# Loading k as float32 beside q, casting it on VectorE and ScalarE, and giving chunks 14 to 17 to transposing transfers

## The chip, the cores and the metric

The kernel runs on one core of a Trainium2 chip. The core has a matrix engine (TensorE, PE in the profile, with its weight loads shown as PEld), a vector engine (VectorE, DVE), a scalar engine (ScalarE, ACT), a general engine that here also issues the loads (GpSimd, POOL), and SyncE (SP), which issues stores and transposing transfers. Sixteen DMA engines move the data. The metric is the device time of one execution in microseconds (us).

## The reference

Inputs: q, k and v of shape (8 batches, 8 heads, 576 positions, 64) and two weight matrices, 512 x 2048 and 2048 x 512, all float32. A retention layer (attention without softmax, with a decay for each head) is followed by a feed-forward block with the Mish activation.

```python
scores = scale * np.matmul(q, k.transpose(0, 1, 3, 2))          # scale = 1/sqrt(64)
gamma = 1.0 - 2.0 ** (-5.0 - np.arange(H))
Dmat = np.where(rel >= 0, gamma[:, None, None] ** rel, 0.0)     # rel = i - j
ret = scores * Dmat
x = np.matmul(ret, v)           # then (batch, position, head * 64): 4608 x 512
h = x @ w_in
out = (h * np.tanh(softplus(h))) @ w_out                        # 4608 x 512, float32
```

## The kernel before

**Chunks and tiles.** The 4608 positions are cut into 36 chunks of 128. Chunks 0 to 7 are the first 128 positions of each batch. From chunk 8 on they come for two batches at a time: three chunks of 128 of the one, three of the other, and one chunk that joins the last 64 positions of both (chunks 14, 21, 28, 35). Four chunks make a tile of 512 positions, so there are nine tiles, t = 0 to 8. Matrix products take bfloat16 inputs and sum in float32.

**Retention by chunk.** A decay is split into a factor for the row (`gq`, which scales q) and one for the column (`gv`, which scales v), so that inside a chunk only a 0/1 mask remains and everything before the chunk goes through a running state of k times v. A chunk n >= 8 passes these steps:

- `load` (L253): GpSimd issues the loads of q (into `qraw`, float32), k (into half of `qks`; this transfer casts float32 to bfloat16 on the way) and v (into `vraw`, float32). One semaphore serves every eighth load, and a load waits until the one eight places before it has landed.
- P, `step_p` (L271): VectorE multiplies q by `gq` and writes bfloat16 into the other half of `qks`.
- V, `step_v` (L276): GpSimd multiplies v by `gv` into `vs`.
- T, `step_t` (L282): `qks` is transposed into `qkT`. For n < NPE (18) TensorE makes eight 128 x 128 transposes into a PSUM buffer `sc`, and ScalarE copies them out (L288, L289). From chunk 18 on a transposing transfer issued by SyncE does it (L291).
- S, `step_s` (L294): TensorE makes the scores of the chunk, VectorE masks them into `sm` (L305).
- `state` (L319): TensorE adds one chunk's k times v to the state (L333), VectorE copies it out as `ssb` (L336). For the first chunk of a batch the k comes from `k0`, which `load_k0` (L247) loads with a cast by the transfer, in eight buffers.
- O, `step_o` (L343): TensorE applies state and scores; VectorE copies the result into the tile's input `xT` (L362).

**Feed-forward.** `g1` (L366) makes one of sixteen 128-wide slices of the hidden layer for a tile: four matmuls into `hp`, a PSUM buffer of which there are two, then Mish on ScalarE. `g2` (L375) makes a quarter of the second product for one chunk, four matmuls. Its sum is in `hp` or in `ops`, a single buffer. `store` (L420) copies it to `res` on VectorE (L422), and SyncE stores it.

**Order.** Every engine works through its own instructions in the order in which the program writes them; nothing is reordered. The first chunks (tiles 0 and 1) have their own path up to about 50 us. Then a loop over u = 0 to 23 (L529) runs the slices of tile 1 with the steps of chunks 8 to 13 between them: P at u = 0, 4, 8, 12, 16, 20 and T at u = 3, 7, 11, 15, 19, 22. The main loop (L563) then runs t = 2 to 9 with sixteen iterations i, in two halves of eight (w = 0 to 7), each half for two chunks n and n + 1, n = 12, 14, 16 and so on: S of the two at w = 0, O at w = 4. P and T of the chunks that follow stand in two places. While they are transposed by TensorE, P of chunks n + 2 and n + 3 is at w = 1 and 3 and T at w = 5 and 6. When they go by transfer, P of n + 4 and n + 5 is at w = 7, and T of n + 2 and n + 3 at w = 0 and 1 of the next half, eight iterations before the S that needs it. In tile t = 2 an iteration has four matmuls of `g1`, and every second one four of `g2`; from t = 3 on it has four of each. Loads run up to five chunks ahead (PF, L47 to L48).

Of the kernel before, what the change touches and what calls it, by code (L numbers as in the profile page):

```python
# [10 lines left out]
F32 = mybir.dt.float32  # L11
BF16 = mybir.dt.bfloat16
AX = mybir.ActivationFunctionType
OP = mybir.AluOpType
# [3 lines left out]
def kernel(  # L18
# [18 lines left out]
    nc = tc.nc  # L37
    B, H, S, D = q.shape
    assert (B, H, S, D) == (8, 8, 576, 64)
    P = 128  # L40
    NP = H // 2
# [2 lines left out]
    nF = d_ff // P  # L44
    KC = d_model // P
    NCH = 4
    NPE = 18  # L47
    PF = 5  # L48


# [11 lines left out]
    consts = ctx.enter_context(tc.tile_pool(name="consts", bufs=1))  # L62
    wpool = ctx.enter_context(tc.tile_pool(name="weights", bufs=1))
    first = ctx.enter_context(tc.tile_pool(name="first", bufs=1))
    io = ctx.enter_context(tc.tile_pool(name="io", bufs=PF))
    tok = ctx.enter_context(tc.tile_pool(name="tok", bufs=5))
    tr = ctx.enter_context(tc.tile_pool(name="tr", bufs=4))
    xp = ctx.enter_context(tc.tile_pool(name="xp", bufs=2))
    gp = ctx.enter_context(tc.tile_pool(name="gp", bufs=2))
    op = ctx.enter_context(tc.tile_pool(name="op", bufs=4))  # L70
# [8 lines left out]
    live = {}  # L79
# [72 lines left out]
    for h in range(H):  # L152
        nc.vector.tensor_scalar(dmask[:, h, :], dist, lg[h], None, op0=OP.mult)
    ex = consts.tile([P, 5, H], F32)
    gq = consts.tile([P, 5, H], F32)
    gv = consts.tile([P, 5, H], F32)
    warm = consts.tile([P, 1], F32)

# [10 lines left out]
    st_sb = {}  # L169
    xts = {}  # L170
    k0 = {}
    v0s = {}


# [7 lines left out]
    def f_transpose(t, g, i, parts):  # L182

        name = ("qb", "kb")[i]
        out_t = first.tile([P, H, P], BF16, name=name + "T", bufs=2)
        n = 8 // len(parts)
        moves = []
        for j, (pool, tname, copy) in enumerate(parts):
            tp = pool.tile([P, 2, 8, P] if tname == "sc" else [P, 8, P], BF16, name=tname)
            tp = (tp[:, 0] if tname == "sc" else tp)[:, 0:n]  # L190
            for r in range(n):
                if t == 1:
                    mix = fst[1][name, "mix", g][:, n * j + r]
                    nc.tensor.transpose(tp[:, r, :], mix.rearrange("p x d -> p (x d)"), ident)
                else:
                    for x in range(2):
                        nc.tensor.transpose(tp[ds(64 * x, 64), r, :],
                                            fst[0][name][:, 2 * g + x, ts(n * j + r, D)], ident)
            moves.append((copy, out_t.rearrange("p h (g r) -> p h g r", r=8)[:, :, :, ds(n * j, n)],
                          tp.rearrange("p r (g h) -> p h g r", h=H)))  # L200
        for copy, to, src in moves:
            copy(to, src)
        fst[t][name, g] = out_t
# [41 lines left out]
        engine.tensor_tensor(v0s[n], v0[n], gv[:, 0, :].unsqueeze(2).to_broadcast([P, H, D]), op=OP.mult)  # L245

    def load_k0(b):  # L247
        k0[b] = first.tile([P, H, D], BF16, name="k0", bufs=B)
        nc.gpsimd.dma_start(out=k0[b], in_=k[b, :, 0:P, :].rearrange("h p d -> p h d"))

    def load(n):  # L253
        if n >= n_chunks:
            return
        b, c = chunks[n]
        qr = io.tile([P, H, D], F32, name="qraw")
        vr = io.tile([P, H, D], F32, name="vraw", bufs=7)
        qks = io.tile([P, 2, H, D], BF16, name="qks", bufs=9)
        live[n] = {"q": qr, "v": vr, "qks": qks}  # L260
        for t, src in ((qr, q), (qks[:, 1], k), (vr, v)):
            if c < 4:
                nc.gpsimd.dma_start(  # L263
                    out=t, in_=src[b, :, ds(P * c, P), :].rearrange("h p d -> p h d"))
            else:
                for e in range(2):
                    nc.gpsimd.dma_start(  # L267
                        out=t[ds(64 * e, 64)],
                        in_=src[b + e, :, ds(512, 64), :].rearrange("h p d -> p h d"))

    def step_p(n):  # L271
        c = chunks[n][1]
        nc.vector.tensor_tensor(live[n]["qks"][:, 0], live[n]["q"],  # L273
                                gq[:, c, :].unsqueeze(2).to_broadcast([P, H, D]), op=OP.mult)

    def step_v(n):  # L276
        c = chunks[n][1]
# [4 lines left out]
    def step_t(n):  # L282
        flat = live[n]["qks"].rearrange("p i h d -> p (i h d)")
        qk = tr.tile([P, 2, NP, P], BF16, name="qkT", bufs=5)
        if n < NPE:
            tp = ps_sc.tile([P, 4 * NP, P], BF16, name="sc")[:, 0:2 * NP]
# [32 lines left out]
    def state(upto):  # L319

        if upto >= n_chunks or done[0] > state_of[upto]:
            return False
        b, c = states[done[0]]
        done[0] += 1
        if c == 0:
            ks, vs = k0[b], v0s[b]
            st_ps[b] = ps_st.tile([P, NP, 64], F32, name="st")
        else:
            ks, vs = live[index[b, c]]["qks"][:, 1], live[index[b, c]]["vs"]
        st = st_ps[b]  # L330
        for p in range(NP):
            for e in range(2):
                nc.tensor.matmul(st[ds(64 * e, 64), p, :], lhsT=ks[:, 2 * p + e, :], rhs=vs[:, 2 * p + e, :],  # L333
                                 start=(c == 0 and p == 0), stop=True, skip_group_check=True)
        ssb = tr.tile([P, 2, NP, 64], BF16, name="ssb", bufs=6)
        nc.vector.tensor_tensor(  # L336
            ssb.rearrange("p e n d -> p e (n d)"),
            st.rearrange("p n d -> p (n d)").unsqueeze(1).to_broadcast([P, 2, NP * 64]),
            diag.unsqueeze(2).to_broadcast([P, 2, NP * 64]), op=OP.mult)
        st_sb[b, c] = ssb  # L340
        return True
# [51 lines left out]
    def stores():  # L393
        while ready:
            store(*ready.pop(), nc.vector.tensor_copy)
# [24 lines left out]
    def store(t, s, ops, copy):  # L420
        ot = op.tile([P, d_model], F32, name="res")
        copy(ot, ops)  # L422
        b, c = chunks[NCH * t + s]
        if c < 4:
            nc.sync.dma_start(out=out[ds(b * S + P * c, P), :], in_=ot)
        else:
            for e in range(2):
                nc.sync.dma_start(out=out[ds((b + e) * S + 512, 64), :], in_=ot[ds(64 * e, 64), :])

    def att(n, steps):  # L430
        if n >= n_chunks:
            return
        for step in steps:
            {"P": step_p, "V": step_v, "T": step_t, "S": step_s, "O": step_o}[step](n)
# [65 lines left out]
    for i in range(nF):  # L500
        for step in steps.get(i, "").split():
            n = int(step[1])
# [17 lines left out]
    def more_loads(upto):  # L520
        for _ in range(2):
            if queued[0] <= upto:
                load(queued[0])
                queued[0] += 1
# [3 lines left out]
    att(N0, "PV")  # L528
    for u in range(24):  # L529
        j, w = divmod(u, 4)  # L530
        if w == 0 and j > 0:
            att(N0 + j, "PV")
            if j < 5:
                if j == 4:
                    load_k0(2)
                load(N0 + j + 3)
            else:
                more_loads(N0 + j + PF)
                load_k0(3)
        elif w == 1 and j > 0:  # L540
            if j > 3:
                state(N0 + j - 1)
            if j < 5:
                att(N0 + j - 1, "S")
            if j < 4:
                state(N0 + j - 1)
            if j > 1:
                att(N0 + j - 2, "O")
            if j == 4:
                state(N0 + j - 1)  # L550
            stores()
        elif w == 2 and 0 < j < 5:
            f_state(1, j - 1, nc.vector)
        elif (w == 3 and j < 5) or (w == 2 and j == 5):
            att(N0 + j, "T")
        stores()
        if u < nF:
            g1(1, u)
        else:
            g2(1, u - nF)  # L560


    for t in range(2, nT + 1):  # L563
        for i in range(nF):
            n, w = NCH * (t + 1) + i // 8 * 2, i % 8
            if t in (3, 4) and i in (4, 12):
                load_k0(2 * t - 2 + i // 8)
            by_pe = n + 2 < NPE
            if w == 0:
                stores()  # L570
                state(n + 1)
                att(n, "S")
                att(n + 1, "S")
            if w == 4:
                state(n + 3)
                stores()
                att(n, "O")
                att(n + 1, "O")
                state(n + 3)
            if by_pe and w in (1, 3):  # L580
                att(n + 2 + w // 2, "P")
            if w in (0, 1):
                att(n + 2 + w, "V")
            if w in (4, 5):
                more_loads(n + w - 2 + PF)
            if w - (5 if by_pe else 0) in (0, 1):
                att(n + 2 + (w == 1 or w == 6), "T")
            if w == 7 and n + 4 >= NPE:
                att(n + 4, "P")
                att(n + 5, "P")  # L590
            stores()
            if t < nT:
                g1(t, i)
            if t == 2:
                if i % 2:
                    g2(1, 8 + i // 2)
            elif t < nT or i < 12:
                g2(t - 1, i)
# [32 lines left out]
```

## Time and profile before

| what | value |
|---|---|
| runs | 312.92 us median of 3 (312.32 to 312.98) |
| the profiled execution | 313.61 us, of which the span of the profile is 311.9 us |
| PE busy | 300.3 us, 96% of the span |
| DVE, ACT, POOL busy | 137.1, 110.7, 143.6 us |
| granted TensorE clock | full in every slice |
| DMA | 42.85 MB in 73642 packets |
| loads by GpSimd (q0) | 48640 packets, 27.27 MB, 61.1% of 16 engines' span |
| transfers by SyncE (q1) | 24832 packets, 15.08 MB, 23.3% |

Times in the views count from the start of the span. A group's line gives the source line, engine, operation, what is written and read, and the number of instructions; a timeline's line gives start, duration and the idle time before. "DMA to landing" is the time from the issue of a transfer to the semaphore that tells of its end.

### The profile page before, as it was taken

Reading aid. Unit: us, or ns where it says so; the run is one execution under the profiler, and the core shown is the slowest. Engines: PE = TensorE matmul, PEld = TensorE weight load, DVE = VectorE, ACT = ScalarE, POOL = GpSimd, SP = SyncE. Lnnn points to the kernel's source line nnn. Section 1 sums busy time; section 2 is a strip of 40 time slices with the busy share of each in tenths; the row PEclk is TensorE's granted clock in tenths of the full one; section 3 lists DMA queues with packets and bytes.
Section 4 is the critical chain, followed back from the end, with each engine's and each line's share of the span. In section 5 each row is a group of like instructions: output and inputs, shape, how many; then the busy total and the mean of one; then the engine's idle time right before and its main releaser. Section 6 shows DMA issues by size and latency. Waiting matters only on the chain.

```text
span 311.9 us, 5809 instructions
## 1 busy us (share of the span) xinstructions
PE 300.3 (96%) x2429; PEld 152.3 (49%) x2468; DVE 137.1 (44%) x200; ACT 110.7 (36%) x183; POOL 143.6 (46%) x178
## 2 busy tenths in 40 slices
PE   7769999999999999999999999999999999999995
PEld 3444554555465554545454444545454544444444
DVE  4723455778637635443434453535354332001111
ACT  4546345671453623233333333232323333333300
POOL 8578849989985976274726262612010000000000
PEclk9999999999999999999999999999999999999999
DMA  7999999999995999999996949371504100010031
GB/s 177 234 206 205 220 208 221 256 171 175 232 203 96 148 181 191 155 195 146 179 178 116 189 88 218 77 144 37 101 36 101 36 34 36 35 34 34 36 101 68
DMA packets 73642, 42.85 MB, mean 137 GB/s; under 512 B 58640, under 2 KB 64528, under 8 KB 73616
## 3 DMA queue, kind: packets, MB, share of 16 engines
q0 software_dynamic: 48640, 27.27, 61.1%
q1 hardware_dynamic: 24832, 15.08, 23.3%
q8 instruction: 19, 0.31, 0.5%
q10 hardware_dynamic: 144, 0.13, 0.1%
q14 instruction: 7, 0.06, 0.1%
HBM read 38.80 MB, written 9.44 MB: 155 GB/s over the span
## 4 chain that ended last, share of the span: by engine, by line
PE 92%; issue 2%; DMA 2%; POOL 2%; DVE 0%; ACT 0%; POOLq 0%; ACTq 0%
PE hp L371 39%; PE ops L386 30%; PE hp L386 4%; PE sc L301 3%; PE st L333 3%; DMA gT<-in_v_dram 2%; PE hp L403 2%; PE sc L353 2%; PE sc L358 2%; PE sc L288 1%; PE st L403 1%; PE ops L403 1%; PE hp L414 1%; POOL gT L106 1%; POOL vb L222 1%
## 5 line engine op out<-in xcount | busy, mean ns | idle before, releaser
L371 PE MATMUL hp<-xT,w_in_t 128*128 128x512 bf16 (+1 forms) x562 | 141.3, 373 | 2.2 <-DVE xT L239 0.8
L373 ACT ACTIVATE gT<-hp 128x512 bf16<-128x512 f32 (+1 forms) x148 | 86.8, 586 | 156.4 <-PE hp L371 144.2
L386 PE MATMUL ops<-w_out_t,gT 128*128 128x512 bf16 x430 | 110.1, 379 | 0.4
L371 PEld LDWEIGHTS <-w_in_t 128*128 128x128 bf16 x592 | 55.1, 98 | 61.9 <-DVE xT L239 1.3
L386 PEld LDWEIGHTS <-gT 128*128 128x128 bf16 x496 | 48.2, 98 | 58.1 <-issue 0.8
L422 DVE COPY res<-ops 128x512 f32<-128x512 f32 x28 | 19.3, 688 | 82.7 <-PE ops L386 79.7
L279 POOL TENSOR_TENSOR vs<-vraw,gv 128x512 bf16<-128x512 f32 x28 | 30.3, 1096 | 51.8 <-PE sc L358 37.6
L336 DVE TENSOR_TENSOR ssb<-st,diag 128x512 bf16<-128x512 f32 x32 | 21.9, 685 | 47.2 <-PE st L333 47.2
L305 DVE TENSOR_TENSOR sm<-sc,mask 128x1024 bf16<-128x1024 f32 x28 | 33.0, 1215 | 6.2 <-PE sc L301 6.2
L263 POOL DMA_DIRECT2D qraw<-in_q_dram x24 | 21.8, 910 | 12.8 <-DVE qks L273 9.6
L263 POOL DMA_DIRECT2D vraw<-in_v_dram x24 | 21.8, 908 | 2.9 <-DMA vpair<-in_v_dram 1.5
L263 POOL DMA_DIRECT2D qks<-in_k_dram x24 | 21.8, 906 | 1.3 <-DMA w_out_t<-in_moe_w_out_dram 0.9
L273 DVE TENSOR_TENSOR qks<-qraw,gq 128x512 bf16<-128x512 f32 x28 | 20.2, 758 | 0.0
L362 DVE CAST xT<-sc 128x512 bf16<-128x512 f32 x24 | 15.3, 680 | 0.0
L386 PE MATMUL hp<-w_out_t,gT 128*128 128x512 bf16 x61 | 14.7, 379 | 0.2
L289 ACT COPY qkT<-sc 128x1024 bf16<-128x1024 bf16 x10 | 10.1, 1010 | 8.0 <-PE sc L288 8.0
L215 DVE TENSOR_TENSOR sm<-sc,dmask 128x1024 bf16<-128x1024 f32 x8 | 9.4, 1220 | 5.0 <-PE sc L211 5.0
L353 PE MATMUL sc<-qkT,ssb 128*64 128x128 bf16 (+1 forms) x224 | 9.5, 213 | 0.0
L358 PE MATMUL sc<-sm,vs 128*64 128x128 bf16 x192 | 9.4, 219 | 0.0
L301 PE MATMUL sc<-qkT 64*128 64x128 bf16 x224 | 9.0, 218 | 0.0
L403 PEld LDWEIGHTS <-gT 128*128 128x128 bf16 x64 | 5.8, 98 | 6.5
L267 POOL DMA_DIRECT2D qraw<-in_q_dram x8 | 5.6, 706 | 7.3 <-DVE qks L273 7.3
(103 smaller groups left out, 192.0 us busy)
## 6 DMA issues: line engine op xcount, KB each, us to landing
out_dram<-res SPq DMA_DIRECT2D x31, 256.0 KB, 3.0
qraw<-in_q_dram POOLq DMA_DIRECT2D x24, 256.0 KB, 6.0
vraw<-in_v_dram POOLq DMA_DIRECT2D x24, 256.0 KB, 6.8
qks<-in_k_dram POOLq DMA_DIRECT2D x24, 128.0 KB, 6.4
w_in_t<-in_moe_w_in_dram POOLq DMA_DIRECT2D x4, 512.0 KB, 11.1
w_out_t<-in_moe_w_out_dram POOLq DMA_DIRECT2D x4, 512.0 KB, 9.8
gT<-in_q_dram SPq DMA_DIRECT2D x4, 256.0 KB, 4.9
gT<-in_k_dram POOLq DMA_DIRECT2D x8, 128.0 KB, 6.3
```

The source lines that it names most:

```text
L263: nc.gpsimd.dma_start(out=t, in_=src[b, :, ds(P * c, P), :].rearrange("h p d -> p h d"))
L273: nc.vector.tensor_tensor(live[n]["qks"][:, 0], live[n]["q"], gq[:, c, :].unsqueeze(2).to_broadcast([P, H, D]), op=OP.mult)
L279: nc.gpsimd.tensor_tensor(vs, live[n]["v"], gv[:, c, :].unsqueeze(2).to_broadcast([P, H, D]), op=OP.mult)
L301: nc.tensor.matmul(sc[:, e, p, :], lhsT=qk[r, 1, p, :], rhs=qk[r, 0, p, :], start=True, stop=True)
L305: nc.vector.tensor_tensor(sm.rearrange("p e n i -> p (e n) i"), sc.rearrange("p e n i -> p (e n) i"), m.unsqueeze(1).to_broadcast([P, 2 * ...
L336: nc.vector.tensor_tensor(ssb.rearrange("p e n d -> p e (n d)"), st.rearrange("p n d -> p (n d)").unsqueeze(1).to_broadcast([P, 2, NP * 64 ...
L353: nc.tensor.matmul(ot[ds(64 * e, 64), p, ds(i0, iw)], lhsT=st_sb[bb, cc][:, e, p, :], rhs=qk[:, 0, p, ds(i0, iw)], start=(i0 == 0 and p == ...
L371: nc.tensor.matmul(hp[:, cols], lhsT=w_in_t[:, c, ts(f, P)], rhs=xts[t][:, c, cols], start=(c == 0), stop=(c == KC - 1))
L373: nc.scalar.activation(gts[t][:, f, cols], hp[:, cols], AX.Mish)
L386: nc.tensor.matmul(ops, lhsT=gts[t][:, f, ts(s, P)], rhs=w_out_t[:, f, :], start=(f == 0), stop=(f == nF - 1))
L403: nc.tensor.matmul(outs[0, s], lhsT=gts[0][:, f, ts(s, P)], rhs=w_out_t[:, f, :], start=(f == 0), stop=(f == nF - 1))
L422: copy(ot, ops)
```

## The change

The loads of k no longer cast. For chunks from 8 on, k lands as float32 beside q in one tile `qkraw`, and P on VectorE multiplies both in one instruction: q by `gq`, k by ones, from a table `gqk`; the result is the bfloat16 `qks`. For the first chunks, k lands as float32 in `k0r`, and ScalarE casts it into `k0` (`cast_k0`). NPE goes from 18 to 14: the transposes of chunks 14 to 17 become transfers, their T moves to w = 0 and 1, and all P of chunks from 14 on are made ahead (14 and 15 at u = 23, the others at w = 7). The transposed tiles of the first chunks share the ring of `qkT`.

```diff
-    NPE = 18
+    NPE = 14
...
-    gq = consts.tile([P, 5, H], F32)
+    gqk = consts.tile([P, 5, 2, H], F32)
+    nc.vector.memset(gqk, 1.0)
+    gq = gqk[:, :, 0, :]
...
-        out_t = first.tile([P, H, P], BF16, name=name + "T", bufs=2)
+        out_t = tr.tile([P, 2, NP, P], BF16, name="qkT", bufs=5).rearrange("p i n t -> p (i n) t")
...
     def load_k0(b):
-        k0[b] = first.tile([P, H, D], BF16, name="k0", bufs=B)
-        nc.gpsimd.dma_start(out=k0[b], in_=k[b, :, 0:P, :].rearrange("h p d -> p h d"))
+        k0r[b] = first.tile([P, H, D], F32, name="k0r", bufs=2)
+        nc.gpsimd.dma_start(out=k0r[b], in_=k[b, :, 0:P, :].rearrange("h p d -> p h d"))
+
+    def cast_k0(b):
+        k0[b] = first.tile([P, H, D], BF16, name="k0", bufs=3)
+        nc.scalar.copy(k0[b], k0r[b])
...
-        qr = io.tile([P, H, D], F32, name="qraw")
+        qkr = io.tile([P, 2, H, D], F32, name="qkraw")
         vr = io.tile([P, H, D], F32, name="vraw", bufs=7)
-        qks = io.tile([P, 2, H, D], BF16, name="qks", bufs=9)
-        live[n] = {"q": qr, "v": vr, "qks": qks}
-        for t, src in ((qr, q), (qks[:, 1], k), (vr, v)):
+        live[n] = {"qk": qkr, "v": vr}
+        for t, src in ((qkr[:, 0], q), (qkr[:, 1], k), (vr, v)):
...
     def step_p(n):
         c = chunks[n][1]
-        nc.vector.tensor_tensor(live[n]["qks"][:, 0], live[n]["q"],
-                                gq[:, c, :].unsqueeze(2).to_broadcast([P, H, D]), op=OP.mult)
+        qks = io.tile([P, 2, H, D], BF16, name="qks", bufs=7)
+        nc.vector.tensor_tensor(qks.rearrange("p i h d -> p (i h) d"),
+                                live[n]["qk"].rearrange("p i h d -> p (i h) d"),
+                                gqk[:, c].rearrange("p i h -> p (i h)").unsqueeze(2).to_broadcast([P, 2 * H, D]),
+                                op=OP.mult)
+        live[n]["qks"] = qks
...
     for u in range(24):
         j, w = divmod(u, 4)
+        if u in (3, 12):
+            cast_k0(u // 12)
...
         elif (w == 3 and j < 5) or (w == 2 and j == 5):
             att(N0 + j, "T")
+        elif w == 3:
+            for n in (NPE, NPE + 1):
+                att(n, "P")
...
+    cast_at = {12: 2, 14: 3, 18: 4, 20: 5, 22: 6, 24: 7}
...
-            by_pe = n + 2 < NPE
+            if w == 2 and n in cast_at:
+                cast_k0(cast_at[n])
...
-            if by_pe and w in (1, 3):
-                att(n + 2 + w // 2, "P")
...
-            if w - (5 if by_pe else 0) in (0, 1):
-                att(n + 2 + (w == 1 or w == 6), "T")
-            if w == 7 and n + 4 >= NPE:
+            if w in (0, 1):
+                att(n + 2 + w, "T")
+            if w == 7:
                 att(n + 4, "P")
                 att(n + 5, "P")
```

More of the change, by code (lines that the diff above doesn't have):

```diff
@@ L171 @@
     k0 = {}
+    k0r = {}
     v0s = {}
```

## The prediction

> **What bounds the kernel now.** I read the page first, then the waits of TensorE, then the timeline of TensorE where the transposes stand, and then the transfers, because both halves of the change end in the transfers.
>
> ```profile
> PE 300.3 (96%) x2429; PEld 152.3 (49%) x2468; DVE 137.1 (44%) x200; ACT 110.7 (36%) x183; POOL 143.6 (46%) x178
> ...
> PE 92%; issue 2%; DMA 2%; POOL 2%; DVE 0%; ACT 0%; POOLq 0%; ACTq 0%
> ```
>
> TensorE is the bound, and the chain that ended last runs through it for 92% of the span. The waits of TensorE say that almost nothing holds it up today:
>
> ```profile
> PE st L236 <- POOL vb L222: 1.7, 1, 1.7
> ```
>
> It is the longest of six waits, and all lie in the first 20 us, which the change leaves alone. So each instruction that leaves TensorE is a gain at its full issue time, and each new wait of TensorE is a loss at its full length. Here is one half of tile 2, with the eight transposes of a chunk between matmuls:
>
> ```profile
> 101.31 0.61 PE L288 MATMUL sc<-ident,qks 128*128 128x128 bf16 x8
> 101.75 1.03 PE L371 MATMUL hp<-xT,w_in_t 128*128 128x512 bf16 x4
> ```
>
> **What is removed.** From the first transpose at 101.31 to the next matmul at 101.75 are 0.44 us. Four chunks make 4 x 0.44 = 1.8 us off the path. Their four ScalarE copies (L289, 1.01 us each) were beside other work, so they bring nothing. This is the whole gain.
>
> **P on VectorE.** P doubles from 512 to 1024 elements. L273 takes 0.68 us now; the nearest row for 1024 elements is L305 with 1.22 us, so I add 0.53 us for each of 28, 15 us in all on an engine that is 44% busy. By itself that costs nothing while VectorE has idle time before its next copy; where it hasn't I count it below. One L273 took 1.53 us, at 58.56, while GpSimd's V ran from 58.05 for 1.49 us instead of 1.07; so 2.1 us is the upper bound for a P that meets a V.
>
> [...]
>
> **Casts on ScalarE.** The nearest row is the ScalarE cast of L222, two in 1.14 us, so 0.57 us each, eight in all. Six stand in the main loop, where ScalarE idles over a microsecond between Mish instructions. The first is worse placed, at u = 3, ahead of the copy of chunk 8's transposes, which ran from 54.14 to 55.15; its S starts at 55.71. With 0.57 us more, the copy ends at 55.72, and I count 0.2 us (0 to 0.4).
>
> **Loads of k.** They now land 256 KB instead of 128 KB. What that costs is read where loads queue up behind each other, by issue plus time to landing of q, k and v of chunk 9:
>
> ```profile
> L263 POOL DMA_DIRECT2D qraw<-in_q_dram x1: 922/922/922, 38.8 to 38.8; - x1
> ...
> DMA to landing us min/median/max: 11.8/11.8/11.8
> ...
> L263 POOL DMA_DIRECT2D qks<-in_k_dram x1: 884/884/884, 40.6 to 40.6; - x1
> ...
> DMA to landing us min/median/max: 10.8/10.8/10.8
> ...
> L263 POOL DMA_DIRECT2D vraw<-in_v_dram x1: 882/882/882, 43.0 to 43.0; - x1
> ...
> DMA to landing us min/median/max: 9.5/9.5/9.5
> ```
>
> q lands at 50.6, k at 51.4, v at 52.5, and the next q (issued 45.4, 8.4 us) at 53.8: the cast k takes 0.8 us of the queue, a float32 load about 1.2. So I add 0.4 us for each k. The bounds are 0.45 above, and below zero beneath, since the read stays at 256 KB and the cast's small packets go. I stay with 0.4, because the rows of q and v are the same transfer. Between 35 and 76 us the queue is never empty. The k of chunk 15 was issued at 71.3 and took 4.8 us, so it landed at 76.1; ahead of it, itself included, are eight k of chunks and three `k0`, so it now lands at 76.1 + 11 x 0.4 = 80.5.
>
> [...]
>
> **P of chunks 14 and 15, moved to u = 23.** They now stand on VectorE ahead of the copy of the last sum that `g2` left in `hp`:
>
> ```profile
> 76.67 0.68 DVE L362 CAST xT<-ops 128x512 bf16<-128x512 f32 x1
> 79.70 0.69 DVE L422 COPY res<-hp 128x512 f32<-128x512 f32 x1 [2.35 <-ACT qkT L289]
> ```
>
> The idle 2.35 us would just hold two P. But chunk 15's waits for its k until 80.5, ends at 81.7, and the copy then ends at 82.3. Its `hp` is the one that the second `g1` of tile 2 needs at 80.34 + 0.86 = 81.2. TensorE waits 1.1 us (0 to 1.9, the upper end with a P that meets a V). The mask, `ssb`, and the store on SP queue behind the same P; O comes four iterations later and still finds them done.
>
> **Four more transposing transfers.** What such a pair costs beside loads, and without:
>
> ```profile
> L291 SPq DMA_TRANSPOSE qkT<-qks x2: 1231/2160/3090, 108.0 to 111.3; - x2
> ...
> DMA to landing us min/median/max: 9.5/10.4/11.3
> ...
> L291 SPq DMA_TRANSPOSE qkT<-qks x2: 1259/1273/1287, 204.3 to 205.7; - x2
> ...
> DMA to landing us min/median/max: 3.2/3.3/3.5
> ```
>
> The later of chunks 18 and 19 lands at 111.3 + 11.3 = 122.6, so the pair takes 14.6 us from the first issue. Two halves on (issues at 123.9 and 125.4, the later 11.0 us to landing) it takes 12.5, then (140.1 and 141.6, 9.4) 10.9, and with no load about, at 204.3, 205.7 + 3.2 - 204.3 = 4.6. The first two pairs are the nearest rows, since loads stand as thick from 80 to 104 us; the bounds are 10.9 and 14.6, and 4.6 if the lighter packets free the queue.
>
> Now the room. A half of tile 2 is short: S of chunks 12 and 13 starts at 79.79, of 14 and 15 at 93.15, of 16 and 17 at 106.61. On SP the first transfer waits behind the store whose copy ends at 82.3, so it is issued at about 82.4, and the pair lands at 95.0 to 97.0. The second of the two S, 0.3 us after the first, would start at 93.45 - 0.9 (one chunk pair's transposes gone) + 1.3 (the waits so far) = 93.85. TensorE waits 1.2 to 3.1 us; I take 2.2. For chunks 16 and 17 the store ahead comes after P of 16 and 17, whose last k is itself late; I put the issue at about 95.4, so landing at 107.9 to 110.0, against 106.9 - 1.8 + 3.5 = 108.6: 0 to 1.4 us, 0.6 taken. Chunks 18 and 19 have 15 us already today (S at 122.78) and are the tightest after that; there TensorE is late by as much as the transfers are, so I take nothing, with 1.5 us as the upper bound. Later pairs meet fewer loads and have 15.7 us.
>
> The rest costs nothing: the `gqk` memset is 0.06 us on VectorE (L127's row), while the start waits for loads until 17 us; the shared `qkT` ring and the smaller `qks` and `k0` rings are read out two steps before they come round. Of the casts, the second finds its k 0.8 us early (landed at 62.1, plus six times 0.4; ScalarE is there at 65.3), and the fourth, at about 96 us, is behind a load of 85.3 + 14 x 0.4 = 90.9, before the transfers take their share. I count nothing for them; late, they hold Mish and so TensorE, and they belong to the worst case below.
>
> **The sum.** -1.8 + 0.2 + 1.1 + 2.2 + 0.6 = +2.3 us. Against the profiled execution's 313.61 us that is 315.9; that execution lies 0.7 us over the runs' median of 312.92, so for the median 315.2.
>
> **Rivals.** *The transfers are hidden, and the gain stands (faster).* If k as float32 takes the queue no longer than the cast did, because the small packets of 36 casting loads go (of 73642 packets 58640 are under 512 B, and the GpSimd queue holds 61.1% of the engines' time), then chunk 15's k lands at 76, P fits into the 2.35 us, and the transfers go out at 80.9. It decides at the pair's time: 93.4 - 0.9 - 80.9 = 11.6 us. Under that, all that is left is -1.8 + 0.2: 311.3. For it speaks the pair at 140 us with 10.9; against it the 1.2 and 0.8 us of the queue, and 14.6.
>
> [...]
>
> *The transfers fall behind for good.* If each pair in tiles 2 and 3 takes the full 14.6 us and loads fall back under them, then P of 18 and 19, ahead of the `res` copy that frees the single `ops`, waits too: -1.8 + 0.4 + 1.9 + 3.1 + 1.4 + 1.5 = +6.5, or 319.4.
>
> **How the numbers follow.** The forecast, new waits outweighing the transposes by 1 to 4 us, has 0.58; the clean gain 0.26; cancelling 0.08; falling behind 0.08. The likeliest one's own range is 313.9 to 317.2. For 8 in 10 the range reaches down past the clean gain (311.1 with the cast at nothing, less 0.4 for the runs' own spread of 0.7), to 310.7, and up to 318.6, short of the full fall. Two runs of this kernel can be told apart from about 0.2%, 0.6 us. Faster by more than that gets the clean gain and a little of the cancelling, 0.27; within it 0.07; slower the rest, 0.66.
>
> **What would show it.** In the profile after, L288 has 48 instead of 80 transposes, and L291 22 instead of 18. Right: TensorE waits at L301 for `qkT` near 93 to 96 us, and at L371 for `res` of VectorE near 81; k of chunk 15 lands after 80 us; the spacing of q, k and v is three times 1.2 us; L273 is about 1.2 us. Wrong: a list of TensorE's waits as short as today's, pairs in tile 2 that land within 11.6 us, or a k that lands 0.8 us after its q.

## The result, and the profile after

The changed kernel takes 325.22 us (median of 6, 322.63 to 336.23) against 312.74 us for the kernel before (6 runs, 312.23 to 313.39): 1.036 times as long, 95% interval 1.031 to 1.042. Two of the six executions took 336 us; the medians here include such executions, the ratios leave them out. The profiled execution took 322.98 us, its span is 321.3 us, 9.4 us more than before. The prediction was 315.2 with a range up to 318.6: the sign was right, the size was not.

The page, in its lines on busy time, the granted clock by slice, and the chain that ended last:

```profile
PE 305.2 (95%) x2436; PEld 152.2 (47%) x2436; DVE 155.7 (48%) x201; ACT 111.2 (35%) x187; POOL 143.8 (45%) x178
...
PEclk9799999999997979999999999999999999999999
...
PE 83%; DMA 11%; DVE 3%; issue 1%; SPq 0%; DVEq 0%
```

TensorE has 32 transposes less to make (the weight loads, PEld, count them: 2468 before, 2436 now; some matmul records of before are missing) and is busy 4.9 us longer. It ran slower for a time: slices 13 and 15 of the granted clock, 96 to 104 and 112 to 120 us, show a 7. (Slice 2 lies in the head.) In the chain, transfers have risen from 2% to 11%. The waits of TensorE give the names:

```profile
PE sc L312 <- DMA qkT<-qks: 7.1, 2, 3.7
...
PE hp L382 <- DVE res L433: 1.3, 1, 1.3
...
PE st L344 <- DVE ssb L347: 0.4, 1, 0.4
```

S (now L312) waits twice for a transposing transfer, and a `g1` once for the `res` copy. TensorE's timeline at the first of the two S:

```profile
93.08 0.40 PE L312 MATMUL sc<-qkT 64*128 64x128 bf16 x8
97.22 0.40 PE L312 MATMUL sc<-qkT 64*128 64x128 bf16 x8 [3.75 <-DMA qkT<-qks]
97.55 3.45 PE L382 MATMUL hp<-xT,w_in_t 128*128 128x512 bf16 x8
```

S of chunk 14 at 93.08, S of chunk 15 at 97.22 after 3.75 us of idleness, and then eight matmuls of `g1` in 3.45 us, where eight take 1.9 us otherwise. The windows view over the stretches behind the two waits (columns: window, its length, busy time of PE, PEld, DVE, ACT, POOL, then the granted clock, the DMA share and GB/s):

```profile
98.10:100.90 2.80, 2.80 (x8) 0.99 (x7) 0.79 (x1) 0.60 (x1) 1.69 (x3) 0.50 1.02 257
...
114.90:118.00 3.10, 3.06 (x14) 1.23 (x15) 1.23 (x1) 0.54 (x1) 1.91 (x3) 0.50 1.08 229
```

The clock is 0.50: each wait is followed by a stretch at half speed, 97.74 to 101.15 and 114.81 to 118.22, 3.41 us each. The second wait's transfers, by their line on SP:

```profile
L302 SPq DMA_TRANSPOSE qkT<-qks x2: 1329/4981/8633, 94.4 to 95.8; - x2
...
DMA to landing us min/median/max: 14.4/16.8/19.1
```

The pair for chunks 16 and 17 needs 95.8 + 19.1 - 94.4 = 20.5 us; the longest pair that the kernel before showed took 14.6.

**Where the time went.** The starts of S in TensorE's timeline cut both profiles at the same work:

| from S to S of chunks | before, us | after, us | difference | what lies in it |
|---|---|---|---|---|
| 8 to 12 | 24.08 | 24.54 | +0.5 | the wait for `ssb`, 0.4 |
| 12 to 14 | 13.36 | 13.92 | +0.6 | two chunks' transposes gone, -0.9; the wait for `res`, +1.3 |
| 14 to 15 | 0.24 | 4.14 | +3.9 | the wait for chunk 15's transfer |
| 15 to 16 | 13.22 | 13.94 | +0.7 | transposes, -0.9; half clock, +1.6 |
| 16 to 17 | 0.24 | 3.78 | +3.5 | the wait for chunk 17's transfer |
| 17 to 18 | 15.93 | 17.49 | +1.6 | half clock |
| 18 to the end of PE | 185.95 | 185.39 | -0.6 | nine halves at 15.93 instead of 16.02 us |

In all +10.2 us. The profiled spans differ by 9.4, since S of chunk 8 itself came 1.1 us earlier here and the end 0.3 us later. That head isn't the change's: in kernels with the same program up to there its S started between 53.7 and 57.8 us. So the experiments below are read from S of chunk 8 on where a microsecond matters.

### The profile page after: what moved, and what is told of

Its sections match the earlier page's. It is cut to its first block, busy times and chain, and to the rows that moved or that the text cites. A ratio compares the mean times of both kernels' runs of the same rounds, so it can differ in the third digit from the quotient of the medians.

```text
span 321.3 us, 5792 instructions
## 1 busy us (share of the span) xinstructions
PE 305.2 (95%) x2436; PEld 152.2 (47%) x2436; DVE 155.7 (48%) x201; ACT 111.2 (35%) x187; POOL 143.8 (45%) x178
## 4 chain that ended last, share of the span: by engine, by line
PE 83%; DMA 11%; DVE 3%; issue 1%; SPq 0%; DVEq 0%
PE hp L382 35%; PE ops L397 27%; DMA qkT<-qks 10%; PE hp L397 4%; PE hp L414 2%; PE sc L312 2%; PE st L344 2%; DMA gT<-in_q_dram 2%; PE sc L364 1%; PE sc L369 1%; DVE qks L281 1%; PE st L414 1%; PE ops L414 1%; PE hp L425 1%; PE sc L215 1%
## 5 line engine op out<-in xcount | busy, mean ns | idle before, releaser
L382 PE MATMUL hp<-xT,w_in_t 128*128 128x512 bf16 (+1 forms) x592 | 146.3, 378 | 2.2 <-DVE res L433 1.3
L382 PEld LDWEIGHTS <-w_in_t 128*128 128x128 bf16 x592 | 55.8, 98 | 65.5 <-issue 4.7
L281 DVE TENSOR_TENSOR qks<-qkraw,gqk 128x1024 bf16<-128x1024 f32 x28 | 38.3, 1401 | 1.2 <-DMA qkraw<-in_k_dram 1.2
L270 POOL DMA_DIRECT2D qkraw<-in_q_dram x24 | 21.7, 905 | 17.3 <-DVE qks L281 13.4
L270 POOL DMA_DIRECT2D qkraw<-in_k_dram x24 | 21.2, 884 | 3.6 <-DMA qkraw<-in_q_dram 2.3
L312 PE MATMUL sc<-qkT 64*128 64x128 bf16 x224 | 9.6, 221 | 7.1 <-DMA qkT<-qks 7.1
L312 PEld LDWEIGHTS <-qkT 64*128 64x128 bf16 x224 | 6.4, 95 | 12.3 <-DMA qkT<-qks 7.5
L300 ACT COPY qkT<-sc 128x1024 bf16<-128x1024 bf16 x6 | 6.1, 1011 | 7.1 <-PE sc L299 7.1
## 6 DMA issues: line engine op xcount, KB each, us to landing
w_out_t<-in_moe_w_out_dram POOLq DMA_DIRECT2D x4, 512.0 KB, 10.2
```

Source lines behind the costliest of these rows:

```text
L270: nc.gpsimd.dma_start(out=t, in_=src[b, :, ds(P * c, P), :].rearrange("h p d -> p h d"))
L281: nc.vector.tensor_tensor(qks.rearrange("p i h d -> p (i h) d"), live[n]["qk"].rearrange("p i h d -> p (i h) d"), gqk[:, c].rearrange("p i ...
L312: nc.tensor.matmul(sc[:, e, p, :], lhsT=qk[r, 1, p, :], rhs=qk[r, 0, p, :], start=True, stop=True)
L382: nc.tensor.matmul(hp[:, cols], lhsT=w_in_t[:, c, ts(f, P)], rhs=xts[t][:, c, cols], start=(c == 0), stop=(c == KC - 1))
```

## Experiments

**1. k as float32 alone.** The changed kernel with the old count of TensorE transposes and the old order of P and T.

```diff
-    NPE = 14
+    NPE = 18
...
+            by_pe = n + 2 < NPE
+            if by_pe and w in (1, 3):
+                att(n + 2 + w // 2, "P")
```

> k loaded as float32 with both casts as in the changed kernel, but chunks 14 to 17 transposed by TensorE, with P and T where the kernel before has them. Theory 'transfers' (the loss is TensorE waiting for transposing transfers in tile 2, and the half clock behind each such wait): no wait for qkT over 1 us, no half-clock stretch after 20 us, 312 to 314 us, that is the time of before plus the 0.2 to 0.5 us of the first ScalarE cast. Rival 'loads' (the heavier loads of k delay everything, the transfers are only where it shows): at least half of the 10 us of loss is still there, 318 us or more, with waits for qkT at chunks 18 to 21. Rival 'VectorE' (the doubled P holds copies that TensorE needs): a wait of TensorE for res or xT of over 1 us.

315.04 us (10 runs, 311.72 to 320.19), ratio 1.001 (0.996 to 1.005); the profiled execution took 312.03. TensorE waits for no `qkT`, and the clock is full. From S of chunk 8 to the end of PE it has 253.1 us, the kernel before 253.0: what the casts and loads cost up to chunk 12 (0.6 us, the wait for `ssb` among it) comes back in the later halves. The median lies 1 us above the expected range, the profiled execution in it; against the kernel before no loss can be told. So the first half of the change is no loss by itself.

**2. The transfers alone.** The kernel before, its k cast by the load, with the four chunks given to transfers.

```diff
-    NPE = 18
+    NPE = 14
...
+        elif w == 3:
+            for n in (NPE, NPE + 1):
+                att(n, "P")
```

> The kernel before with chunks 14 to 17 transposed by transfers and P of 14 and 15 at u = 23, k still cast by its load. Theory 'transfers': the pair of 14 and 15 takes 12 to 15 us from its first issue (about 81 us), so TensorE waits 1 to 4 us at its S and again at 16 and 17, with at least one half-clock stretch: 314 to 320 us. Rival 'loads': the pairs take 11 us or less, no wait, 311 us (the 1.8 us of transposes gained). In both the 1.3 us wait for res near 80 us is gone, since P is 0.7 us.

322.42 us (4 runs, from 322.1), ratio 1.028 (1.021 to 1.034), 2 us over the expected range. Its waits of TensorE, and the timeline behind the longer one:

```profile
PE sc L301 <- DMA qkT<-qks: 7.3, 2, 7.0
```

```profile
112.80 0.61 PE L301 MATMUL sc<-qkT 64*128 64x128 bf16 x8 [7.00 <-DMA qkT<-qks]
113.34 1.89 PE L371 MATMUL hp<-xT,w_in_t 128*128 128x512 bf16 x4
115.02 1.91 PE L386 MATMUL ops<-w_out_t,gT 128*128 128x512 bf16 x4
```

Four matmuls take 1.7 us instead of 0.87: half clock, here 6.8 us of it (110.7 to 117.6). The transfers carry most of the loss alone. With k cast by the load the pair of 14 and 15 took 11.9 us and that of 16 and 17 took 19.0.

**3. The matmuls that keep the clock up.** The changed kernel with 16 matmuls on zeros (3.5 us) between S of chunks 14 and 15, and of 16 and 17.

```diff
                 att(n, "S")
+                if n in (14, 16):
+                    keep_warm(16, ps_h, "hp")
                 att(n + 1, "S")
```

> The changed kernel with 16 matmuls on zeros (3.45 us at full clock, into a spare hp buffer, read by nobody) put between S of 14 and S of 15, and between S of 16 and S of 17. Theory 'idle halves the clock': the waits of 3.7 and 3.4 us shrink to under 0.6 us because TensorE works meanwhile, the granted clock stays at 1.0 from 20 us on, and the time falls by what the two half-clock stretches cost, 2 x 1.7 = 3.4 us, against the changed kernel on the same chip: about 319 to 320 us. Rival 'the clock falls for another reason' (load, heat, the transfers themselves): the two stretches of 3.4 us at 0.5 remain, and the time is that of the changed kernel within 1 us.

324.48 us (5 runs, from 320.86), ratio 1.029 (1.021 to 1.037). The interval overlaps that of the changed kernel, 1.031 to 1.042: the gain of 3.4 us was not there to be seen. In the profiled execution, one of 331.53 us, the filling left 1.1 us of the wait at chunk 15, and the clock stayed up. But the pair of 16 and 17 took 29.1 us: S of chunk 16 waited 3.26 us, with the clock still full behind it (16 matmuls in 3.63 us), and S of chunk 17 5.75 us behind its filling, with half clock.

```profile
112.61 0.40 PE L312 MATMUL sc<-qkT 64*128 64x128 bf16 x8 [3.26 <-DMA qkT<-qks]
112.94 3.63 PE L170 MATMUL hp<-zeros 128*128 128x512 bf16 x16
122.32 0.61 PE L312 MATMUL sc<-qkT 64*128 64x128 bf16 x8 [5.75 <-DMA qkT<-qks]
```

The same kernel once more:

> The changed kernel with 16 matmuls on zeros between S of chunks 14 and 15, and between S of 16 and 17, once more, for a profile of the filled waits. Theory (a saving at the first filled wait is taken up by the next wait, since that ends when a transfer lands, whenever TensorE comes to it): waits of 15 and 17 together no shorter than 7.1 us with the matmuls counted in, no half clock behind them unless a third wait comes; time 1 to 2 us below the changed kernel's, 321 to 323. Rival (each of the two stretches at half clock is a cost of its own): 3.4 us below, 319.5 to 320.

329.39 us (6 runs, from 324.85), ratio 1.046 (1.039 to 1.052), 6 us over the upper end of what was expected. In the profiled execution the pairs took 23.8 and 25.6 us, longer than without filling, so S of chunk 15 waited 9.2 us behind its filling, and half clock followed. At chunk 17 the filling covered the wait, and from S of chunk 17 to 18 are 15.95 us, as in the kernel before, against 17.49 without filling. So the filling does what it should where it covers the wait, and the total tells nothing, because the transfers' length moves it by more. That a saving at the first wait is taken up by the second was neither shown nor refuted. The same with one wait only, on experiment 2:

```diff
+                if n == 16:
+                    keep_warm(28, ps_h, "hp")
```

> The transfers alone again (as in e2_t_only: NPE 14, k cast by its load, P of chunks 14 and 15 at u = 23), with 28 matmuls on zeros (0.216 us each, 6.0 us in all) put between S of chunk 16 and S of chunk 17. There TensorE waited 7.0 us for chunk 17's transfer, and was at half clock until 4.75 us after the wait's end. The added matmuls change no data; they lie in the wait. Theory (the half clock is a cost of its own that comes on top of the wait, and in this kernel nothing later takes it up): the wait that is left is some 1 us, the clock stays full, the transfer lands as late as before, and the time falls by 4.75 / 2 = 2.4 us, to 319.7 (319.0 to 320.4). Rival (the wait alone is the cost, or a later wait takes up what is saved): 322.1 to 322.7, as without the matmuls.

325.82 us (6 runs, from 323.37), ratio 1.039 (1.033 to 1.046): again the total missed. In its timeline the clock is up behind the wait:

```profile
109.32 6.22 PE L167 MATMUL hp<-zeros 128*128 128x512 bf16 x28
116.31 0.40 PE L301 MATMUL sc<-qkT 64*128 64x128 bf16 x8 [0.77 <-DMA qkT<-qks]
116.64 1.04 PE L371 MATMUL hp<-xT,w_in_t 128*128 128x512 bf16 x4
```

S of 17 to S of 18 is 15.94 us against 18.22 in experiment 2: 2.3 us less, as expected (2.4). What made up for it: S of chunk 8 was 1.9 us later (a stretch at lower clock in the head), chunk 15's transfer was waited for 1.9 us instead of 0.3, and the pair of 16 and 17 took 20.6 us instead of 19.0. These two kernels ran on another chip than experiments 1 to 3, the one of the kernels with a gate in every half, below; whether that or the filling makes the pairs longer is open.

**4. A pause by itself.** The kernel before with a matmul, a chain of ScalarE copies, and a matmul that needs the last of them, in tile 7, where little is loaded (DMA share 0.16 about the short pause); two copies, then seven.

```diff
+            if t == 7 and i == 2:
+                src = ps_h.tile([P, d_model], F32, name="hp")
+                nc.tensor.matmul(src, lhsT=ident, rhs=w_out_t[:, 0, :], start=True, stop=True)
+                lag = op.tile([P, d_model], BF16, name="lag", bufs=1)
+                nc.scalar.copy(lag, src)
+                for j in range(1):          # 6 in the long one
+                    nc.scalar.copy(lag, lag)
+                hp = ps_h.tile([P, d_model], F32, name="hp")
+                nc.tensor.matmul(hp, lhsT=lag[:, 0:P], rhs=w_out_t[:, 0, :], start=True, stop=True)
```

> The kernel before, with one pause of TensorE put in at tile 7, slice 2, where nothing else is late: a matmul, two ScalarE copies of 512 elements one behind the other (0.6 us each), and a matmul that needs the last. It adds two matmuls (0.22 us each) and a pause of some 1.5 us. Theory (a wait under about 3 us costs its own length and leaves the clock full): about 2.0 us over the kernel before (1.6 to 2.4), granted clock full in every slice. Rival (each pause, however short, is followed by a half-clock stretch): 3.7 us or more, with a slice at less than full clock behind it.

315.03 us against 312.88 for the kernel before, ratio 1.006 (1.002 to 1.010). The timeline, first of the short pause and then of the long one:

```profile
239.97 0.39 PE L600 MATMUL hp<-w_out_t,lag 128*128 128x512 bf16 x1 [1.33 <-ACT lag L598]
240.19 1.03 PE L371 MATMUL hp<-xT,w_in_t 128*128 128x512 bf16 x4
```

> The same with seven copies in the chain instead of two, so a pause of some 4.5 us. Theory (a wait of over 3.4 us is followed by a stretch of 3.41 us at half clock, which costs 1.7 us more than the wait): 4.5 + 0.4 + 1.7 = 6.6 us over the kernel before (6.1 to 7.1), and one stretch at a granted clock near 0.5 behind the pause. Rival (the half-clock stretch in the records costs no time): 4.9 us over it.

321.49 us (4 runs), ratio 1.026 (1.018 to 1.033), 2 us more than expected.

```profile
246.28 0.61 PE L600 MATMUL hp<-w_out_t,lag 128*128 128x512 bf16 x1 [4.57 <-ACT lag L598]
246.68 1.91 PE L371 MATMUL hp<-xT,w_in_t 128*128 128x512 bf16 x4
248.38 1.91 PE L386 MATMUL ops<-w_out_t,gT 128*128 128x512 bf16 x4
250.09 1.91 PE L371 MATMUL hp<-xT,w_in_t 128*128 128x512 bf16 x4
```

A wait of 1.33 us leaves the matmuls at 1.03 us; one of 4.57 us is followed by half clock until 252.1. From the first added matmul to the next `state` are 5.48 and 11.60 us: 6.12 more, of which 3.25 are the longer pause and 2.87 the half clock. The sign was as expected, the size (1.7) was not: the stretch was 6.8 us long, of which about 1 lay in the pause. Both rivals (that every pause does it, that it costs nothing) are out.

**5. Loads held back until a pair has landed.** First at one place, in the changed kernel: before it issues the loads of chunks 18 to 20, GpSimd reads a column of chunk 15's `qkT` (a gate, below).

```diff
+            if n == 12 and w == 4:
+                gate = consts.tile([P, 1], BF16)
+                nc.gpsimd.tensor_copy(gate, live[15]["qk"][:, 0, 0, 0:1])
```

> The changed kernel, but GpSimd reads one column of chunk 15's transposed tile before it issues the loads of chunks 18 to 20, so that these loads start only when the pair of 14 and 15 has landed. Theory 'transfers slow down beside loads': the pair takes 6 to 9 us instead of 14.7, and S of 15 does not wait (under 0.5 us); the delayed loads then lie beside the pair of 16 and 17, whose wait stays at 3 us or more. Time 317 to 321. Rival 'the transfers are slow by themselves or held on SP': the pair still takes over 12 us and the wait at S of 15 stays near 3.7 us.

334.84 us (4 runs, 328.47 to 350.94; too scattered for a ratio). In its one profile, of an execution of 336.05 us, the pair of 14 and 15 took 8.5 us, and S of 15 did not wait. The loads that were put off then lay beside the next pair, which took 20.4 us. So the wait was moved, and the total is a miss. Next, the same in every half, on the transfers alone (experiment 2):

```diff
+    gate = consts.tile([P, 1], BF16)
...
+            if w == 4 and max(12, NPE - 2) <= n < 28:
+                nc.gpsimd.tensor_copy(gate, live[n + 3]["qk"][:, 0, 0, 0:1])
...
-            if w in (4, 5):
+            if w == 4 or (w == 5 and n > 12):
```

> Chunks 14 to 17 by transfers with k cast by its load (as in e2_t_only), but in every half of the main loop up to chunk 27 GpSimd reads one column of the later transposed tile before it issues the next loads, and the first half of tile 2 issues two chunks of loads instead of three. Theory 'transfers slow down beside loads': every pair lands within 6 to 10 us of its first issue, no wait for qkT over 0.5 us, no half-clock stretch, and the 1.8 us of transposes is gained: 311 to 312 us, 1 to 2 us under the kernel before on the same chip. Rival 'the transfers need that long with any traffic, and loads pushed together fall behind': waits stay, or move to P (VectorE waiting for q, TensorE for res): 314 us or more.

310.65 us (10 runs, 309.92 to 311.64), ratio 0.9925 (0.9902 to 0.9948): faster than both kernels. The pair of chunks 16 and 17 here:

```profile
L291 SPq DMA_TRANSPOSE qkT<-qks x2: 1488/1529/1570, 91.9 to 93.5; - x2
...
  POOL gate L571: 4.6, 1
...
DMA to landing us min/median/max: 3.5/3.9/4.2
```

The same pair that took 19.0 us now takes 5.2; nobody waits for it but GpSimd's `gate`. From S of chunk 8 to the end of PE are 251.2 us, 1.8 less than before: the transposes, and nothing else.

Two things limit what this shows. The loads that a gate holds back lie beside the next pair: 18 and 19 took 11.9 us and 20 and 21 took 15.0, where 6 to 10 were expected, and chunk 21's transfer landed only 0.2 us ahead of its S. And the loads themselves ran faster in this kernel, long before the first gate (at 85.0 us). Chunk 8's q, k and v landed at 42.6, 43.4 and 44.1, in experiment 2 at 46.5, 47.4 and 48.7; chunk 15's k at 69.4 and 76.3. The v of chunk 8, here and then in experiment 2 (the times to landing are of its q, k and v):

```profile
L263 POOL DMA_DIRECT2D vraw<-in_v_dram x1: 901/901/901, 35.6 to 35.6; - x1
...
DMA to landing us min/median/max: 8.6/8.7/8.8
```

```profile
L263 POOL DMA_DIRECT2D vraw<-in_v_dram x1: 901/901/901, 37.3 to 37.3; - x1
...
DMA to landing us min/median/max: 10.9/11.0/11.3
```

So no load was outstanding when the first pair was issued here, where experiment 2 had five. Up to the first gate the program is that of experiment 2, apart from the small tile that a gate writes. The two kernels of experiment 7 have loads as close together, and the other eleven profiles have them further apart, among them two on the same chip (experiment 6, and the filled form of experiment 2). The cause is open, so what the gates would have brought without it is not shown.

**6. The changed kernel with the same gates.**

```diff
+    gate = consts.tile([P, 1], BF16)
...
+            if w == 4 and max(12, NPE - 2) <= n < 28:
+                nc.gpsimd.tensor_copy(gate, live[n + 3]["qk"][:, 0, 0, 0:1])
...
-            if w in (4, 5):
+            if w == 4 or (w == 5 and n > 12):
```

> The changed kernel (k as float32) with the same ordering of loads behind transfers, two chunks of loads in the first half of tile 2. Theory 'transfers slow down beside loads': no wait for qkT over 0.5 us; what is left over e5_t_gated is the wait for res near 80 us (P of 2 us each), 0.5 to 1.4 us, and the first cast: 312 to 313.5 us. Rival 'loads': the float32 k keeps the queue so full that pairs or P still come late: 316 us or more.

318.08 us (4 runs, from 317.13), ratio 1.015 (1.009 to 1.021).

```profile
PE sc L312 <- DMA qkT<-qks: 6.4, 2, 5.5
```

So it came out as the rival 'loads' had it, 316 us or more. The pair of 14 and 15 took 12.5 us, and that of 20 and 21 took 20.8 with a wait of 5.5. Five loads were outstanding when the first pair was issued, where experiment 5 had none. That goes with the longer loads (here chunk 8's v landed 1.2 us after its k) and not with the form of k alone, as experiment 2, with casts, had five too. The later pair got its loads from the gate itself: GpSimd had waited 6.24 us for the pair of 18 and 19, which landed at 120.6, and then sent off a `k0r` load and six chunk loads (121.2 to 126.5), just as the pair of 20 and 21 was issued (121.9).

```profile
120.68 0.19 POOL L585 COPY gate<-qkT 128x1 bf16<-128x1 bf16 x1 [6.24 <-DMA qkT<-qks]
121.21 0.93 POOL L253 DMA_DIRECT2D k0r<-in_k_dram  x1 [0.34 <-issue]
```

With the same gates the two forms of k are 7.4 us apart, but the loads of experiment 5 also took less time, so this can't be put down to the form of k. Without gates they are 2.8 apart (325.22 and 322.42), with intervals of the ratios that overlap.

**7. The gates without more transfers**, and with half of them: the kernel before with gates (NPE 18), and with NPE 16.

```diff
-    NPE = 18
+    NPE = 16        # in the second of the two only
...
+    gate = consts.tile([P, 1], BF16)
...
+            if w == 4 and max(12, NPE - 2) <= n < 28:
+                nc.gpsimd.tensor_copy(gate, live[n + 3]["qk"][:, 0, 0, 0:1])
```

> The kernel before, with nothing changed but the loads of tiles 3 to 6 held until the pair of transposing transfers of that half has landed. Theory 'transfers slow down beside loads': the pairs of chunks 18/19 and 20/21 take 6 to 10 us instead of 14.6 and 12.5; the time is that of before within 0.5 us, since TensorE did not wait there. Rival: the pairs take as long as before.

311.84 us (10 runs), ratio 0.9953 (0.9928 to 0.9978). The pair of 18 and 19 takes 5.3 us instead of 14.6. From S of chunk 8 on nothing is gained (253.0 us), as the pair was waited for by nobody; what is gained lies ahead of it, where the programs are the same: the loads land as close together as in experiment 5, and S of chunk 8 came at 53.7 us instead of 55.7. Why is open.

> The kernel before with only chunks 16 and 17 moved to transfers (half of the transposes, 0.9 us of TensorE), k cast by its load, loads held behind the transfers from the second half of tile 2 on. Theory: pair of 16/17 in under 11 us because the three chunks of loads before it have mostly landed, no wait over 0.5 us, 0.9 us under before: about 312. Rival: the loads still in flight at 93 us hold the pair beyond 12 us and S of 17 waits 1 us or more.

311.49 us (10 runs), ratio 0.9951 (0.9923 to 0.9978); from S of chunk 8 on 252.3 us, 0.7 less, near the 0.9 of two chunks' transposes. The pair of 16 and 17 took 6.6 us.

**Pairs of the runs**, from issue and landing of each transfer and load (experiments by number):

| kernel | chunks | loads outstanding at the first issue | loads issued until the landing | pair, us |
|---|---|---|---|---|
| 2 with gates | 14, 15 | 0 | 0 | 5.7 |
| 2 with gates | 16, 17 | 3 | 0 | 5.2 |
| before with gates | 18, 19 | 0 | 0 | 5.3 |
| changed, one gate | 14, 15 | 5 | 0 | 8.5 |
| transfers alone | 14, 15 | 5 | 10 | 11.9 |
| before | 18, 19 | 3 | 10 | 14.6 |
| changed | 14, 15 | 4 | 11 | 14.7 |
| transfers alone | 16, 17 | 8 | 13 | 19.0 |
| changed | 16, 17 | 8 | 14 | 20.5 |
| 2 with gates | 18, 19 | 6 | 2 | 11.9 |
| 2 with gates | 20, 21 | 4 | 3 | 15.0 |
| changed with gates | 14, 15 | 5 | 2 | 12.5 |
| changed with gates | 20, 21 | 3 | 6 | 20.8 |
| before | 20, 21 | 7 | 3 | 12.6 |
| changed, filled again | 14, 15 | 4 | 15 | 23.8 |
| changed, filled again | 16, 17 | 8 | 9 | 25.6 |

Over all profiles, 83 pairs had no load issued between their first issue and their landing, and took 4.2 to 9.2 us; the other 60 took 7.9 to 29.1 (though a longer pair also leaves more time to issue loads). But the two counts don't give the length: 3 and 6 went with 20.8 us, 3 and 10 with 14.6.

## Why the prediction was wrong in size

**What held.** The bound (TensorE, no slack), the transposes at 0.44 us a chunk (experiment 5 gives back 1.8 us for four), float32 k at 0.4 us more of the load queue (chunk 8's q, k and v land at 45.96, 47.16 and 48.38, 1.2 us apart, where the casting k landed 0.83 us behind its q), and the place of the waits: S of chunks 15 and 17, and `res` near 82. The first transfer was issued at 82.45, predicted 82.4, but that is luck: S of chunk 8 came 1.1 us early, and the copy ahead of the transfer was late for another reason than reckoned (below). The clean gain is out: both pairs (14.7 and 20.5 us) were longer than the 11.6 us named as the point that decides. So is the cancelling (gain and new waits about equal, 0.08): the three new waits alone came to 8.5 us, against 1.8 gained.

**The step that failed: a pair's length taken as a fixed row.** The prediction took 12.5 to 14.6 us from the first pairs of the kernel before and argued that "loads stand as thick". They did not. At 108.0 us, three loads were outstanding; at 94.35 us, when the pair of 16 and 17 went out in the changed kernel, all eight were, and 14 more came before it landed. The row was a price beside the loads of that place, not of the operation. For chunk 17 the term was 0.6 (0 to 1.4) and the wait 3.4; for chunk 15 it was 2.2 (1.2 to 3.1) and the wait 3.75, since the pair came 0.1 us over the upper row and TensorE got there 0.4 us earlier than reckoned. That the loads make the length is seen in the one gate of experiment 5, which took the first pair from 14.7 to 8.5 us with loads as far apart as before, in the 4.5 and 4.7 us of pairs of the kernel before with no load outstanding or issued (at 221.1 and 236.3 us; at 204.3, the prediction's place for this, five loads were still outstanding), and in the 9.2 us that no pair exceeded beside which no load was issued; the 5.2 to 6.6 us under gates in experiments 5 and 7 had shorter loads to help.

**The term that was missing: the clock behind a wait.** Each of the two waits was priced at its own length. Half clock behind them added 1.6 us each, 3.2 in all, more than the term for chunk 15. The kernel before ran at full clock everywhere, so no row of it showed this. The waits here of 1.33 and 1.92 us (experiment 4, and chunk 15 in the filled form of experiment 2) left the clock up, and so did the one of 3.26 us (chunk 16 in experiment 3); those of 3.38, 3.75, 4.57, 5.5, 5.75, 7.0 and 9.2 us did not. The length alone doesn't decide. The two stretches of the changed kernel start 17.07 us apart, five times 3.41. Counted back in steps of 3.41 us from where its half clock starts (121.12), the wait of 3.26 us (109.35 to 112.61) lies across two such steps with over 1.6 us of work in each; the 3.41 us ahead of each half-clock stretch behind these waits held 0.5 us of work or less. That much is measured; what brings the clock down no run here shows.

**The wait for `res`.** The term was 1.1, the wait 1.3, but the reason was another. Chunk 15's k was to land at 80.5; it landed at 76.1, as before:

```profile
77.40 3.98 DVE L281 TENSOR_TENSOR qks<-qkraw,gqk 128x1024 bf16<-128x1024 f32 x2
81.31 0.68 DVE L433 COPY res<-hp 128x512 f32<-128x512 f32 x1
```

The delay of 0.4 us a load had been made up: chunk 10's q and k landed at 53.8 and 56.7 us in the kernel before, at 54.1 and 55.3 now, so the kernel before lost there, for a reason that was not sought, about what the changed one lost load by load. The copy was late because both P took 2.0 us instead of the 1.2 of most others. No V ran beside them until 80.8 us, so a P that meets a V is not the reason. In experiment 6 the same two took 1.21 each, and the wait was gone. What doubles a P now and then is open.

**Small terms.** The first cast's 0.2 can't be told from the head's spread. P twice as wide was priced at nothing up to the `res` copy; the wait for `ssb`, 0.4 us at 70.8 us, comes behind a P that took 2.57 us (in experiment 1, 0.5 us behind one of 2.69); in the other kernels with k as float32 that P took 2.2 us or less, and the wait is not there. And the tail's -0.6 was foreseen by nobody: in the kernels with k as float32 a half from chunk 18 on takes 15.93 us, in those with a casting load 16.02. Its cause wasn't sought.

**The sum.** Predicted: -1.8 + 0.2 + 1.1 + 2.2 + 0.6 = +2.3. Measured from S of chunk 8: -1.8 + 0.4 (`ssb`) + 1.3 + 3.75 + 3.4 + 3.2 - 0.6 = +9.7, against 10.2 from the starts. The rival that falls behind, 319.4, was nearest, and right in that the pairs fall behind; it, too, lacked the clock and capped a pair at 14.6, and its waits behind P of 18 and 19 didn't come.

## What to carry to other kernels

The time of a transfer read in one place (here a pair's 14.6 us at 108.0 us in the kernel before) holds for the loads about it at that place (at 94.35 us in the changed kernel a pair took 20.5): count the transfers outstanding when it is issued and those that follow before it lands, and where it is to move to a thicker place, take a longer time than the longest row. Price a new wait of the bound engine at its length only while it is short (1.33 and 1.92 us left the clock full here); waits of 3.4 us and more cost 1.6 to 2.9 us more here in lost clock. And holding loads back until a pair had landed made that pair faster here (8.5 us instead of 14.7), but put the loads beside the next one (20.4 us): in the kernel whose loads landed 0.7 to 0.8 us apart anyway this went with a gain of 0.75%, 1.8 us of it the transposes; in the one where they landed 1.2 us apart it left a wait of 5.5 us.

## What the runs showed that was not expected

- A pair of transposing transfers takes 4.5 and 4.7 us with no load outstanding or issued in the kernel before (5.4 and 6.2 in the changed one), 5.2 to 6.6 us at four places under gates where loads land 0.7 to 0.8 us apart, 8.5 under a gate where they land 1.2 us apart, and up to 29.1 us beside loads.
- Half clock lasted 3.41 us behind waits of 3.38, 3.75 and 5.5 us, 6.8 us behind waits of 4.57, 5.75 and 7.0 us, and 10.2 us behind one of 9.2 us. The 3.41 us ahead of the first stretch in the changed kernel (94.33 to 97.74) were not wholly idle: they hold 0.5 us of work, S of chunk 15 and the start of the `g1` behind it.
- With one program up to that point, a float32 load of 256 KB landed 0.8 us behind the load before it in three kernels, and 1.3 us behind it in the other five with casting loads (v of chunk 8). The kernel with gates that had loads 1.2 us apart, and k as float32, took 7.4 us longer than the one with loads 0.7 to 0.8 us apart and the casting k.
